# Which steps keep their G in PSUM: one fixed set against a set by the kind of half round

## The chip, the cores and the metric

The kernel runs on one core of a Trainium2 chip. The metric is the device time of one execution in microseconds; the time before is the median of three runs. The rows below come from one further execution, taken by the hardware profiler.

## What is computed

Agent attention followed by a feed-forward layer, all in float32. With `scale = 1/sqrt(128)` and B = 2, N = 12480 rows, C = 128, 49 agents, 2048 hidden units:

```python
def sm(a, b):
    s = scale * (a @ b.transpose(0, 2, 1))
    s = s - s.max(-1, keepdims=True)
    e = np.exp(s)
    return e / (e.sum(-1, keepdims=True) + 1e-09)
agent_v = sm(agents, k) @ v
x = (sm(q, agents) @ agent_v).reshape(B * N, C)
h = x @ w_in
g = np.where(h > 0.0, h, np.exp(np.minimum(h, 0.0)) - 1.0)
out = g @ w_out
```

## The kernel before

**Stages.** A prologue of some 57 us computes k's scores, the maximum, the exponentials and `agent_v` of the first batch and converts the weights. Then comes the main loop, which is the rest. It runs over S = 416 steps. A round is 960 rows of q (26 rounds, 13 in each batch); it has two half rounds of 480 rows, and a half round has NP = 8 steps, one for each 256 of the 2048 hidden units. So there are 52 half rounds, counted here from 0.

**One step s.** `p1` (L400) makes H for this step on TensorE, six matmuls of 480 columns into a tile `h` of two PSUM banks. `elu` (L411) computes `e = exp(h - 1)` on ScalarE (L414) and G = max(min(e, 1), h) on VectorE (L416). `split` (L419), called for the step before, splits G into two float32r parts for the product with `w_out`: `hi` on ScalarE (L202) and `lo = G - hi` (L207). `p2` (L432) is issued four steps later (LAG = 4), twelve matmuls that add into the two output banks; its last four pairs read `lo`.

**Kept steps.** If `is_kept(s)`, G is written back over H in the PSUM tile, and `lo` is one VectorE operation of 960 columns; the PSUM tile is then in use until that operation has ended. GpSimd reads only SBUF here, so in the other steps G goes to an SBUF tile `g` (three of them), the PSUM tile is free once VectorE has written G, and `lo` is two GpSimd operations of 480 columns. Before, steps 1, 3 and 6 of every half round are kept.

**PSUM tiles.** Two of the eight banks take the output, and six are three tiles of two banks that `slot` (L140) hands out. Everything else that needs PSUM in the main loop takes one of the same three.

**What else stands in a half round.** The next rounds' attention is spread over the steps by `plan` and `at` (L655, L474). A *visit* computes two pieces (scores of q, scores of k, or products with v) in one tile, which ScalarE and VectorE then read. Visits stand at step 1 (early) or at step 3 (late, EDGE = 3). Late ones are in half rounds 0, 1, 3, 5, ... 19, then 21, 25, 29, ... 45; early ones in 2, 4, ... 16. The transposes of the softmax of q (`q_ring`, L353) take a tile at step 6 of the even half rounds 2 to 48 (in half round 1 at step 4), which ScalarE (L346) and VectorE (`px`, L207) read. In half rounds without a late visit `p1` of step 5 is issued ahead, at step 4. The maximum over k takes a tile at step 5 of half round 8 and one at step 0 of half round 9. In half rounds 9 to 17 and 19, the maximum is subtracted (`e_sub`, L211, VectorE) or exponentials are taken for the second batch.

**Order.** Every engine runs its instructions in the order in which the loop at L724 issues them: in step s first `p1(s)`, then `p2(s - 4)`, `elu(s)`, `split(s - 1)`, and last the visit or the transposes of this step. The output is moved to HBM by SP's queue, which also loads the inputs.

Of the kernel before, what the change touches and what calls it, by code (L numbers as in the profile page):

```python
# [24 lines left out]
def tile_agent_attention_moe(  # L25
# [25 lines left out]
    LEAD = 6  # L51
    NP = NM // 2
    EDGE = (NP - 1 + LAG) % NP
    KEPT = (1, 3, 6)
    scale = 1.0 / float(C) ** 0.5

    const = ctx.enter_context(tc.tile_pool(name="const", bufs=1))
# [337 lines left out]
        return x // 2, x % 2, c  # L395

    def is_kept(s):
        return s % NP in KEPT

    def p1(s):  # L400
        j, half, c = at_step(s)
# [9 lines left out]
    def elu(s):  # L411

        h, e = h_t.pop(s), x_p.tile([128, 2, T], F32, tag="e", name="e")
        nc.scalar.activation(out=e, in_=h, func=ACTF.Exp, bias=-1.0, scale=1.0)  # L414
        g = h if is_kept(s) else g_p.tile([128, 2, T], F32, tag="g", name="g", bufs=3)
        nc.vector.scalar_tensor_tensor(out=g, in0=e, scalar=1.0, in1=h, op0=ALU.min, op1=ALU.max)  # L416
        g_t[s] = g

    def split(s):  # L419
        if not 0 <= s < S:  # L420
            return
        g = g_t.pop(s)
        hi_t[s] = hi = g_p.tile([128, 2, T], F32R, tag="hi", name="hi", bufs=5)
        lo_t[s] = lo = g_p.tile([128, 2, T], F32R, tag="lo", name="lo", bufs=4)
        cast_hi(nc.scalar, hi, g)
        if is_kept(s):
            rest(nc.vector, lo, g, hi)
        else:
            for i in range(2):
                rest(nc.gpsimd, lo[:, i, :], g[:, i, :], hi[:, i, :])  # L430
# [46 lines left out]
    with tc.manual_schedule():  # L477
# [153 lines left out]
        visits = {}  # L631
# [153 lines left out]
```

## Time and profile before

| | us |
|---|---|
| median of three runs (966.14 to 968.47) | 968.03 |
| the profiled execution | 964.99 |
| its span, first to last instruction | 963.2 |
| TensorE matmuls busy | 939.2 (98%) |
| ScalarE busy | 852.1 (88%) |
| VectorE busy | 786.7 (82%) |
| GpSimd busy | 726.5 (75%) |

Busy shares are means over the whole span, prologue included. The page's granted TensorE clock is 9 (90% or more) in each of its 40 slices. The matmuls of a step come in pairs that start together; the next pair starts 0.22 us later though each matmul is shown with 0.38. In the rows, PE is TensorE's matmuls, PEld its weight loads, DVE VectorE, ACT ScalarE, POOL GpSimd.

### The profile page before, as it was taken

How to read it: one execution, taken by the hardware profiler on the slowest of the kernel's cores; microseconds unless marked ns; L12 is line 12 of the kernel's file. 1: busy time of each engine (PE TensorE's matmuls, PEld its weight loads, DVE VectorE, ACT ScalarE, POOL GpSimd, SP SyncE). 2: the span in 40 equal slices, each digit the busy share in tenths (PEclk: the TensorE clock that was granted, in tenths of full speed). 3: DMA queues.
4: the chain of work that ended last, by engine and by line, in shares of the span. 5: the costliest groups of instructions: out<-in, count | busy, mean ns of one | idle time of the engine just before them, and what ended most of it. 6: DMA issues, size and time to landing. Idle time of an engine off the chain costs nothing.

```text
span 963.2 us, 26620 instructions
## 1 busy us (share of the span) xinstructions
PE 939.2 (98%) x11102; PEld 815.0 (85%) x11102; DVE 786.7 (82%) x897; ACT 852.1 (88%) x1020; POOL 726.5 (75%) x623
## 2 busy tenths in 40 slices
PE   7889999999999999999999999999999999999998
PEld 5778888888888888888888889888989888888886
DVE  7858788788888888888788888888888887888885
ACT  4649989988889889988999998999999999989996
POOL 3336777767877877877887887887878878878886
PEclk9989999999999999999999999999999999999999
DMA  9941222224232211012002101101020020001000
GB/s 347 400 145 55 103 95 78 69 74 121 67 92 82 68 33 59 27 38 73 28 21 69 38 27 53 38 28 63 28 78 28 22 68 31 31 15 38 27 22 21
DMA packets 26195, 67.48 MB, mean 70 GB/s; under 512 B 3239, under 2 KB 15171, under 8 KB 26075
## 3 DMA queue, kind: packets, MB, share of 16 engines
q1 hardware_dynamic: 26075, 65.79, 20.5%
q8 instruction: 87, 1.43, 0.6%
q14 instruction: 33, 0.27, 0.1%
HBM read 43.11 MB, written 12.78 MB: 58 GB/s over the span
## 4 chain that ended last, share of the span: by engine, by line
PE 68%; DVE 5%; ACT 2%; issue 2%; POOL 0%; DVEq 0%; ACTq 0%; POOLq 0%
PE o L444 43%; PE h L408 23%; ACT e L414 2%; PE h L222 1%; DVE g L416 1%; DVE lo L207 1%; DVE h L416 1%; DVE qe L307 1%; DVE mx L299 1%; PE h L332 0%; PE h L294 0%; ACT hi L202 0%; ACT oa L459 0%; DVE ob L456 0%; POOL ob L460 0%
## 5 line engine op out<-in xcount | busy, mean ns | idle before, releaser
L207 POOL TENSOR_TENSOR lo<-g,hi 128x480 fp32r<-128x480 f32 x520 | 627.1, 1238 | 137.7 <-PE h L408 68.5
L414 ACT ACTIVATE e<-h 128x960 f32<-128x960 f32 x416 | 406.1, 976 | 55.5 <-PE h L408 36.8
L416 DVE SCALAR_TENSOR_TENSOR g<-e,h 128x960 f32<-128x960 f32 x260 | 299.1, 1151 | 96.2 <-ACT e L414 94.4
L408 PE MATMUL h<-py,ahi 50*128 50x480 f32 x832 | 261.3, 394 | 5.1 <-DVE qe L307 3.2
L202 ACT ACTIVATE hi<-g 128x960 fp32r<-128x960 f32 x260 | 261.5, 1006 | 1.3 <-DVE g L416 1.3
L408 PE MATMUL h<-px,ahi 50*128 50x480 f32 x832 | 261.6, 394 | 0.9 <-DVE lo L207 0.5
L444 PE MATMUL o<-lo,w_hi 64*128 64x480 f32 x1664 | 255.1, 379 | 0.4 <-POOL lo L207 0.4
L444 PE MATMUL o<-hi,w_lo 64*128 64x480 f32 x1664 | 253.0, 377 | 1.3 <-ACT hi L202 1.3
L444 PE MATMUL o<-hi,w_hi 64*128 64x480 f32 x1664 | 254.3, 378 | 0.0
L416 DVE SCALAR_TENSOR_TENSOR h<-e,h 128x960 f32<-128x960 f32 x156 | 180.8, 1159 | 35.4 <-ACT e L414 31.3
L444 PEld LDWEIGHTS o<-lo,w_hi 64*128 64x128 f32 x1664 | 163.9, 184 | 20.4 <-POOL lo L207 1.2
L444 PEld LDWEIGHTS o<-hi,w_lo 64*128 64x128 f32 x1664 | 164.3, 185 | 19.8 <-ACT hi L202 1.4
L207 DVE TENSOR_TENSOR lo<-h,hi 128x960 fp32r<-128x960 f32 x156 | 179.4, 1150 | 0.0
L444 PEld LDWEIGHTS o<-hi,w_hi 64*128 64x128 f32 x1664 | 164.1, 184 | 17.4
L408 PEld LDWEIGHTS h<-py,ahi 50*128 50x128 f32 x832 | 145.1, 186 | 26.0 <-PE o L444 6.2
L408 PEld LDWEIGHTS h<-px,ahi 50*128 50x128 f32 x832 | 145.2, 186 | 16.7 <-DVE g L416 5.4
L408 PE MATMUL h<-py,alo 49*128 49x480 f32 x416 | 156.9, 377 | 0.0
L408 PE MATMUL h<-px,alo 49*128 49x480 f32 x416 | 156.9, 377 | 0.0
L202 ACT ACTIVATE hi<-h 128x960 fp32r<-128x960 f32 x156 | 151.6, 971 | 0.0
L460 POOL TENSOR_TENSOR ob<-ob,oa 128x480 f32<-128x480 f32 x51 | 63.4, 1243 | 58.6 <-ACT oa L459 38.8
L408 PEld LDWEIGHTS h<-px,alo 49*128 49x128 f32 x416 | 78.1, 188 | 4.9 <-DVE alo L278 0.2
L408 PEld LDWEIGHTS h<-py,alo 49*128 49x128 f32 x416 | 78.2, 188 | 4.7
(98 smaller groups left out, 523.0 us busy)
## 6 DMA issues: line engine op xcount, KB each, us to landing
k<-in_kT_dram SPq DMA_DIRECT2D x26, 480.0 KB
q<-in_qT_dram SPq DMA_DIRECT2D x26, 480.0 KB
out_dram<-ob SPq DMA_DIRECT2D x51, 240.0 KB
v<-in_vx_dram SPq DMA_DIRECT2D x13, 516.0 KB
v<-in_vx_dram SPq DMA_DIRECT2D x13, 483.8 KB
py<-px SPq DMA_DIRECT2D x52, 93.8 KB
py<-px SPq DMA_DIRECT2D x52, 91.9 KB
raw<-in_w_in_dram SPq DMA_DIRECT2D x4, 512.0 KB
```

What stands on the lines that cost most here:

```text
L202: nc.scalar.activation(out=out, in_=x, func=ACTF.Copy)
L207: eng.tensor_tensor(out=out, in0=x, in1=hi.bitcast(F32), op=ALU.subtract)
L222: nc.tensor.matmul(out=ps[u:u + 64], lhsT=e[:, j * NA:j * NA + 64], rhs=v_t[b, r][:, j, :], start=(r == rs[0] and j < 2), stop=(r == rs[-1 ...
L299: nc.vector.tensor_reduce(out=mx, in_=v, axis=AX.X, op=ALU.max)
L307: nc.vector.tensor_tensor(out=e, in0=v, in1=q_st[j]["mx"].unsqueeze(2).to_broadcast([TQ, R, NA]), op=ALU.subtract)
L408: nc.tensor.matmul(out=h[:, u, 0:T], lhsT=a[x, :], rhs=p[u ^ half][x, :], start=i == 0, stop=i == 2)
L414: nc.scalar.activation(out=e, in_=h, func=ACTF.Exp, bias=-1.0, scale=1.0)
L416: nc.vector.scalar_tensor_tensor(out=g, in0=e, scalar=1.0, in1=h, op0=ALU.min, op1=ALU.max)
L444: nc.tensor.matmul(out=o_t[u][:, 0:T], lhsT=w[x], rhs=v[x, :], start=first and i == 0, stop=last and i == len(jobs) - 1)
L460: nc.gpsimd.tensor_tensor(out=ob, in0=ob, in1=oa, op=ALU.add)
```

## The change

The fixed set of kept steps becomes a table by the kind of half round, and `is_kept` looks up the kind: "late" if a visit stands at step 3, else "early" if one stands at step 1, else "turn" in even half rounds (those with transposes and no visit), else none. `visits` is filled before the loop runs. In late half rounds steps 1 and 6 are kept, step 3 no longer; in early and turn half rounds 1, 3 and 7; in the others 1, 3 and 6 as before.

```diff
-    KEPT = (1, 3, 6)
+    KEPT = {"late": (1, 6), "early": (1, 3, 7), "turn": (1, 3, 7), None: (1, 3, 6)}
@@
     def is_kept(s):
-        return s % NP in KEPT
+        first = s - s % NP
+        steps = visits.values()
+        if first + EDGE in steps:
+            kind = "late"
+        elif first + 1 in steps:
+            kind = "early"
+        else:
+            kind = "turn" if first // NP % 2 == 0 else None
+        return s - first in KEPT[kind]
```

## Rows read from the trace of the kernel before

**Rows 1.** The page: busy us, share of the span, instructions, of each engine

```profile
PE 939.2 (98%) x11102; PEld 815.0 (85%) x11102; DVE 786.7 (82%) x897; ACT 852.1 (88%) x1020; POOL 726.5 (75%) x623
```

**Rows 2.** The page: the chain that ended last, shares by engine

```profile
PE 68%; DVE 5%; ACT 2%; issue 2%; POOL 0%; DVEq 0%; ACTq 0%; POOLq 0%
```

**Rows 3.** Half rounds 27, 24, 25: stretch, length, busy us (instructions) by engine

```profile
541.76:557.72 15.96, 15.96 (x146) 13.57 (x146) 13.39 (x14) 15.29 (x19) 12.49 (x11) 1.00 0.12 40
...
491.37:507.51 16.14, 16.14 (x155) 13.59 (x152) 13.43 (x13) 15.66 (x20) 14.72 (x14) 1.00 0.04 16
507.51:525.61 18.10, 17.71 (x274) 15.69 (x274) 15.43 (x18) 16.03 (x20) 13.14 (x12) 1.00 0.29 92
```

**Rows 4.** Half round 25, two q: start, us, engine, operation [idle before, releaser]

```profile
511.48 0.37 PE L408 MATMUL h<-py,ahi 50*128 50x480 f32 x1
...
513.44 0.37 PE L408 MATMUL h<-py,ahi 50*128 50x480 f32 x1
...
516.21 1.15 DVE L416 SCALAR_TENSOR_TENSOR h<-e,h 128x960 f32<-128x960 f32 x1
...
517.02 0.48 PE L408 MATMUL h<-py,ahi 50*128 50x480 f32 x1
...
517.61 2.38 POOL L207 TENSOR_TENSOR lo<-g,hi 128x480 fp32r<-128x480 f32 x2
...
518.92 0.96 ACT L202 ACTIVATE hi<-h 128x960 fp32r<-128x960 f32 x1
...
518.94 0.56 DVE L307 TENSOR_TENSOR qe<-h,mx 124x392 f32<-124x392 f32 x1
...
519.65 0.45 PE L408 MATMUL h<-py,ahi 50*128 50x480 f32 x1 [0.39 <-DVE qe L307]
...
522.67 4.79 POOL L207 TENSOR_TENSOR lo<-g,hi 128x480 fp32r<-128x480 f32 x4 [2.68 <-ACT hi L202]
```

**Rows 5.** What `p1` (L408) waited for, loads and matmuls: us, times

```profile
  DVE px L207: 4.7, 21
...
  DVE qe L307: 3.2, 8
```

**Rows 6.** Half round 1: `p1` of steps 4 and 5

```profile
87.38 0.48 PE L408 MATMUL h<-py,ahi 50*128 50x480 f32 x1
...
90.81 0.48 PE L408 MATMUL h<-py,ahi 50*128 50x480 f32 x1 [0.53 <-DVE g L416]
```

**Rows 7.** The page's costliest groups: count, busy us, mean ns, idle before

```profile
L207 POOL TENSOR_TENSOR lo<-g,hi 128x480 fp32r<-128x480 f32 x520 | 627.1, 1238 | 137.7 <-PE h L408 68.5
...
L408 PE MATMUL h<-py,ahi 50*128 50x480 f32 x832 | 261.3, 394 | 5.1 <-DVE qe L307 3.2
...
L207 DVE TENSOR_TENSOR lo<-h,hi 128x960 fp32r<-128x960 f32 x156 | 179.4, 1150 | 0.0
```

**Rows 8.** Half round 3, q and k: `p1` of steps 4 and 5

```profile
124.67 0.48 PE L408 MATMUL h<-py,ahi 50*128 50x480 f32 x1
...
127.14 0.46 PE L408 MATMUL h<-py,ahi 50*128 50x480 f32 x1 [0.22 <-DVE m_all L171]
```

**Rows 9.** `lo` of steps 4, 5 in half round 24; matmuls reading step 6's

```profile
504.57 4.79 POOL L207 TENSOR_TENSOR lo<-g,hi 128x480 fp32r<-128x480 f32 x4 [0.74 <-POOL lo L207]
...
513.00 0.60 PE L444 MATMUL o<-lo,w_hi 64*128 64x480 f32 x4
```

**Rows 10.** Half round 9: G of step 0, and `p1` of step 1

```profile
226.81 1.14 DVE L416 SCALAR_TENSOR_TENSOR g<-e,h 128x960 f32<-128x960 f32 x1
...
226.94 0.48 PE L408 MATMUL h<-py,ahi 50*128 50x480 f32 x1
```

**Rows 11.** Half round 11: subtractions (L211), and GpSimd's `lo` beside the second

```profile
269.66 0.56 DVE L211 TENSOR_TENSOR s_all<-s_all,mb 120x392 f32<-120x392 f32 x1
...
276.60 1.02 DVE L211 TENSOR_TENSOR s_all<-s_all,mb 120x392 f32<-120x392 f32 x1
...
275.97 5.54 POOL L207 TENSOR_TENSOR lo<-g,hi 128x480 fp32r<-128x480 f32 x4 [2.30 <-ACT hi L202]
```

## The prediction

> **What bounds the kernel now.** I read the page's busy shares first, then the chain that ended last, then the busy time of single half rounds, then the order of time inside a few of them. TensorE is busy 98% of the span [rows 1] and the chain runs through its matmuls [rows 2]. So a microsecond in which TensorE stands still after the prologue is a microsecond of the span, and other engines count only where they make it stand. A half round (8 steps) with nothing in it takes 15.96 us [rows 3]. A plain step is 1.96 us, from one `p1` to the next at 511.48 and 513.44 [rows 4], and 8 of those are 15.7: such a half round has almost nothing to win. One with transposes takes 16.14 and TensorE is busy in all of it. One with a late visit of two q parts takes 18.10, and there TensorE is busy for 17.71, so 0.4 us idle [rows 3].
>
> The idle time has a name. After the late visit at step 3 comes `p1` of step 4 at 517.02, then `p1` of step 5 only at 519.65. That is 2.63 us where 1.96 is plain, and it waits for `qe` (L307), the last reader of the visit's PSUM tile, 518.94 + 0.56 [rows 4]. The three PSUM tiles are handed out by who is released first in program order. With step 3 kept, its tile is released only by its `lo` on VectorE in step 4, so the earliest released tile for step 5 is the visit's own, and its four VectorE operations come behind step 3's `g`. The trace fits that order elsewhere too: the `p1` behind the transposes waits for `px` (L207), their tile's last reader, 21 times [rows 5], and in half round 1, where the transposes come at step 4, step 5 waits for step 4's `g` [rows 6].
>
> **What the change moves.** Of 52 half rounds, 18 have a late visit, 8 an early visit, 17 are "turn", 9 are the rest. The kept steps go from 156 to 18 x 2 + 34 x 3 = 138. Eighteen `lo` leave VectorE (18 x 1.150 = 20.7 us) and come to GpSimd as 36 operations of 1.238 us (44.6 us) [rows 7]. In 25 even half rounds the third kept step moves from 6 to 7, with no change in counts. No DMA is added or moved on SP's queue.
>
> **Late visit without step 3.** I walked the hand-out of tiles through one such half round. The visit still takes step 2's tile, step 4 still takes step 1's (released by step 1's `lo`), but step 5 now takes step 3's, which step 3's `g` releases: 516.21 + 1.15 = 517.36 [rows 4], 1.6 us before it is wanted. The visit's tile goes to step 6, wanted at about 521 and free at 519.50. So the wait goes wholly. The price of one: 2.63 - 1.96 = 0.67, less about 0.1 by which the first matmul after a visit is longer anyway (0.48 at 517.02, 0.37 at 511.48 [rows 4]); I take 0.6. The trace has this wait for `qe` 8 times [rows 5]: 8 x 0.6 = 4.8 us. With q and k the same step waits for the k reduction: 127.14 - 124.67 = 2.47, so 0.51 - 0.1, about 0.45 [rows 8], in half rounds 0, 3, 5 and 7: 1.8 us. In half round 1 the step from 87.38 to 90.81 is 3.43 [rows 6]; less 1.96, 0.1 and 0.2 for the transposes (16.14 - 15.96 [rows 3]), some 1.1 remains, and by the new order both the transposes and step 5 get tiles that are free in time: 1.0 us. The five other late half rounds (11, 13, 15, 17, 19) show no such wait and give nothing. Sum: 4.8 + 1.8 + 1.0 = 7.6 us. The low bound is TensorE's own idle before these: 3.2 for the eight `qe` [rows 5], 0.53 in half round 1 [rows 6], 0.22 for each q and k [rows 8], some 4.6 us.
>
> What hides the added GpSimd work: step 2's `lo` ends at 517.61 + 2.38 = 519.99, step 3's `hi` at 518.92 + 0.96 = 519.88, and GpSimd then stands idle 2.68 us until step 4's `hi` [rows 4]. The new pair, 2.4 us, fits that hole. If it did not, step 4's and 5's `lo` would be late by what sticks out, and `p2` four steps later would wait. In the whole half round GpSimd would be busy 13.14 + 2.4 = 15.5 of about 17.5 us [rows 3].
>
> **Transposes or early visit, step 7 for 6.** Behind the transposes, step 0 of the next half round now takes step 6's tile (released by its `g`, before the transposes' readers), so the wait for `px` goes: 4.7 us of weight loads in 21 places [rows 5]. The loads run ahead of their matmuls, and of those the costliest group of this line shows only 5.1 us idle in all, 3.2 of it `qe` [rows 7]. So the gain lies between 0 and 4.7; I take 1.0, near the low end. GpSimd now has steps 4, 5, 6 in a row: steps 4 and 5 end at 504.57 + 4.79 = 509.36, step 6 would end at 511.8, and the matmuls that read it start at 513.00 [rows 9]: 1.2 us of slack, no stall. VectorE does step 7's `lo` in step 0 instead of step 6's in step 7. It stands behind step 0's `g` there, so `g` of step 1 moves by some 0.3 us, which nobody on TensorE waits for.
>
> One place loses. In half round 9 the second small matmul of the k maximum takes a tile in step 0. It now takes the transposes' tile, and `p1` of step 1 gets step 0's own, so it waits for step 0's `g`. That starts at 226.81 today and could start some 0.25 earlier (its `e` is done by then), ending near 227.65, while `p1` starts at 226.94 [rows 10]: +0.7 us, once.
>
> **Contention.** In the half rounds that subtract the maximum (`s_all`, L211, both inputs in SBUF) one such operation took 0.56 us at 269.66 and another 1.02 at 276.60, in the middle of four `lo` on GpSimd that took 5.54 us [rows 11] where four take 4.79 elsewhere [rows 9]. So they collide, by 0.75 us on GpSimd and 0.46 on VectorE in such a half round, whereas the `lo` of a kept G keeps a mean of 1.15 us and GpSimd's 1.24 [rows 7]. In five late half rounds the added GpSimd pair lies next to those subtractions. TensorE waits for no `lo` there today, so I take 0, and keep half of the 0.75 in each, 5 x 0.4 = 2 us, for the range.
>
> The Trainium skill (SBUF — State Buffer, Who interferes with whom) has the rule: a VectorE instruction with two SBUF inputs and a GpSimd instruction that reads SBUF exclude each other for the whole instruction, while one with at most one SBUF input doesn't contend. By it, moving a `lo` from VectorE, where G came from PSUM, to GpSimd speaks against the change: free work becomes work that can be blocked. The rows agree on both halves of the rule. By it the sum would lose up to the 2 us kept above.
>
> **Sum.** 7.6 + 1.0 - 0.7 = 7.9 us. Against the profiled execution: span 963.2, so 955.3, and its time 964.99 gives 957.1. The median of the runs shown is 968.03, 3.0 above the profiled execution, so I set the sum against the median: 960.1, rounded to 960.
>
> **Rivals.**
> (1) *The stall comes back later in the half round.* After the visit ScalarE has `e`, `hi` and the exponentials of q back to back; were step 5's `e` late, step 6 or 7 would inherit part of the wait. For: ScalarE is busy 16.03 of 18.10 there [rows 3]. Against: the tiles that steps 6 and 7 take are released over 1.5 us before. Half of the 7.6 stays: 964.
> (2) *The change doesn't do what it says:* the tiles are handed out otherwise than I read, so step 5 still gets the visit's. Then 7.6 falls away and the rest nearly cancels: 968. Against: three different waits in the trace fit my reading [rows 4 to 6].
> (3) *GpSimd becomes the bound:* slower. A late half round with an even one after it (18.10 + 16.14 = 34.2 us) holds 13.14 + 14.72 = 27.9 us of GpSimd today, with 2.4 more 30.3 [rows 3], in 22 `lo` operations and others. It decides where one operation takes (34.2 - 30.3) / 22 = 0.18 us above its 1.2. Beside L211 four of them took 5.54, so 1.385 each [rows 11], just there. If the moved `lo` of step 7 collided as L211 does, with 1.45 each (0.25 x 22 = 5.5), the pair would take 35.8, 1.6 more than today, in some 15 pairs: about 992. Against: kept and unkept `lo` run side by side today at their usual times.
>
> **How the numbers follow.** Forecast 960: 0.70, within 956.5 to 963 by the bounds above (4.6 instead of 7.6, 0 to 4.7 for `px`, 2 us of contention). Rival 1, 964: 0.11. Rival 2, 968: 0.11. Rival 3, 992: 0.08. A range from 956.5 to 966 holds the forecast and rival 1, 0.8. A measurement of this kernel tells some 0.3% (2.9 us) from no change. Faster by more: the forecast and nearly all of rival 1, 0.80; within: rival 2 and a little of rival 1, 0.12; slower: 0.08.
>
> **What would show it.** Right: in a late half round with two q parts the step from `p1` 4 to `p1` 5 falls from 2.63 to about 2.07 and the half round from 18.1 to about 17.5; TensorE's wait for `qe` is gone; after transposes the wait for `px` is gone; GpSimd has no hole of 2.7 us after a late visit; `p2` never waits for `lo`. In half round 9 a new wait of some 0.7 us on `g`. Wrong: late half rounds still at 18 us, or `p1`, `p2` waits on GpSimd's `lo`, or GpSimd operations over 1.3 us on the mean.

## The result and the profile after

The changed kernel takes 958.08 us, the median of six runs (956.81 to 961.22), where the kernel before took 967.44 in its six (966.1 to 969.24). The ratio is 0.9908, with a 95% interval of 0.9886 to 0.9930: 8.9 us faster, between 6.8 and 11.0.

The profiled execution of the changed kernel took 960.39 us, its span is 958.6, so the span is only 4.6 us shorter than that of the kernel before (963.2). Where the rest is, the first start of `p1` tells, which ends the prologue. These are the rows for one group of `p1`'s matmuls, before and after (count, ns least/median/most, first and last start in us; line 416 after is line 408 before):

```profile
L408 PE MATMUL h<-px,ahi x832: 372/380/598, 57.3 to 951.8; 50*128 50x480 f32 x84, 49*128 49x480 f32 x83
```

```profile
L416 PE MATMUL h<-px,ahi x832: 372/380/766, 60.6 to 947.2; 50*128 50x480 f32 x84, 49*128 49x480 f32 x83
```

The main loop, from there to the end of the span, took 963.2 - 57.3 = 905.9 us before and 958.6 - 60.6 = 898.0 after: 7.9 us less. The prologue, which the change doesn't touch, was 3.3 us longer in this execution. The last section shows that it varies from execution to execution, and main loops are compared below by this difference.

Half round 0 opens the main loop, and its length varies too, by over 1 us with the same work, as the experiment on the even half rounds shows. These are the stretches behind it, before and after (length, then busy us and instructions of PE, PEld, DVE, ACT, POOL, then clock, DMA share, GB/s):

```profile
77.40:963.20 885.80, 875.73 (x10129) 762.52 (x10125) 732.39 (x788) 810.91 (x951) 701.76 (x591) 1.00 0.17 51
```

```profile
80.83:958.60 877.77, 871.72 (x10129) 768.84 (x10125) 715.08 (x771) 807.68 (x951) 742.66 (x625) 1.00 0.17 52
```

That is 8.0 us less behind half round 0.

On the page after (busy us and share of the span by engine; then the chain that ended last), GpSimd has gained 43 us and VectorE lost 18 against [rows 1], near the 44.6 and 20.7 that were forecast for 36 operations more and 18 fewer:

```profile
PE 939.0 (98%) x11102; PEld 825.1 (86%) x11102; DVE 769.1 (80%) x879; ACT 848.8 (89%) x1020; POOL 769.4 (80%) x659
...
PE 93%; DVE 2%; ACT 2%; POOL 1%; DMA 1%; issue 0%; SPq 0%; DVEq 0%; ACTq 0%; POOLq 0%
```

Over the whole span the busy time of TensorE is the same to 0.2 us, but only because the longer prologue makes up for the rest: behind half round 0 it fell from 875.7 to 871.7 us, and the idle time from 10.1 to 6.1. So half of the 8.0 us was standing still by the profile, and half was shown as busy time. The two shares of matmuls in the chain, 68% [rows 2] and 93%, can't be set side by side: before, the chain could be followed back only to 211.9 us, and its shares add up to 77%. From some 260 us on, where both chains are known, matmuls are about 90% of the one before and all of the one after.

The stretches after, half rounds 25, 24, 27, 9 and 11, in the same columns:

```profile
507.71:525.22 17.51, 17.51 (x275) 16.25 (x273) 14.35 (x17) 15.88 (x20) 15.28 (x14) 1.00 0.29 95
491.62:507.71 16.09, 16.09 (x154) 15.22 (x152) 13.40 (x13) 15.63 (x19) 14.69 (x14) 1.00 0.04 16
541.36:557.24 15.88, 15.88 (x147) 13.97 (x145) 13.40 (x14) 15.24 (x19) 12.54 (x11) 1.00 0.12 40
225.81:243.92 18.11, 17.18 (x212) 14.97 (x210) 14.75 (x19) 15.81 (x20) 13.67 (x12) 1.00 0.45 118
...
262.38:280.23 17.85, 17.85 (x226) 15.11 (x224) 14.95 (x18) 16.23 (x22) 15.55 (x13) 1.00 0.32 92
```

Against [rows 3], the half round with a late visit of two q parts falls from 18.10 to 17.51 and TensorE is busy in all of it; the turn half round and the plain one hardly move (0.05 and 0.08). Inside half round 25 (start, us, engine, operation, idle before):

```profile
516.42 1.15 DVE L424 SCALAR_TENSOR_TENSOR g<-e,h 128x960 f32<-128x960 f32 x1
...
517.26 0.48 PE L416 MATMUL h<-py,ahi 50*128 50x480 f32 x1
...
517.82 9.59 POOL L207 TENSOR_TENSOR lo<-g,hi 128x480 fp32r<-128x480 f32 x8
...
519.14 0.57 DVE L307 TENSOR_TENSOR qe<-h,mx 124x392 f32<-124x392 f32 x1
...
519.33 0.38 PE L416 MATMUL h<-px,ahi 50*128 50x480 f32 x1
...
521.30 0.37 PE L416 MATMUL h<-px,ahi 50*128 50x480 f32 x1
```

Step 5's `p1` now starts at 519.33, 2.07 us after step 4's, while the visit's last reader (`qe`) runs until 519.71: it no longer waits for it. Step 6's, which by the walk has the visit's tile, comes at 521.30, 1.6 us after that. GpSimd has no hole: eight `lo` operations stand in one row where 2.68 us were idle [rows 4], at the same 1.2 us each.

Everything that `p1` waits for after, loads and matmuls together (us, times), in place of [rows 5]:

```profile
its engine sat idle before it (us, times) until:
  DVE g L424: 10.6, 39
  issue: 3.2, 13
  ACT e L422: 1.6, 4
  DVE lo L207: 1.2, 2
  ACT ahi L270: 0.9, 2
  DMA py<-px: 0.5, 1
  DVE alo L278: 0.2, 1
```

The two waits that carried the sum, `qe` (3.2 us, 8 times) and `px` (4.7 us, 21 times), have no row any more. A new one, for a DMA (a copy by the DMA engines), has.

### The profile page after: what moved, and what is told of

It is laid out like the page before. It is cut to its first block, busy times and chain, and to the rows that moved or that the text cites. A ratio compares the mean times of both kernels' runs of the same rounds, so it can differ in the third digit from the quotient of the medians.

```text
span 958.6 us, 26706 instructions
## 1 busy us (share of the span) xinstructions
PE 939.0 (98%) x11102; PEld 825.1 (86%) x11102; DVE 769.1 (80%) x879; ACT 848.8 (89%) x1020; POOL 769.4 (80%) x659
## 3 DMA queue, kind: packets, MB, share of 16 engines
q1 hardware_dynamic: 26075, 65.79, 20.7%
## 4 chain that ended last, share of the span: by engine, by line
PE 93%; DVE 2%; ACT 2%; POOL 1%; DMA 1%; issue 0%; SPq 0%; DVEq 0%; ACTq 0%; POOLq 0%
PE o L452 55%; PE h L416 29%; PE h L222 3%; PE h L294 2%; PE h L163 1%; POOL lo L207 1%; DMA k<-in_kT_dram 1%; PE h L332 1%; DVE g L424 0%; DVE m_all L171 0%; DVE ex L110 0%; PE h L478 0%; ACT ex L106 0%; DMA py<-px 0%; DVE fr L112 0%
## 5 line engine op out<-in xcount | busy, mean ns | idle before, releaser
L207 POOL TENSOR_TENSOR lo<-g,hi 128x480 fp32r<-128x480 f32 x556 | 669.9, 1239 | 82.2 <-ACT hi L202 36.2
L424 DVE SCALAR_TENSOR_TENSOR g<-e,h 128x960 f32<-128x960 f32 x278 | 320.1, 1152 | 122.5 <-ACT e L422 93.7
L202 ACT ACTIVATE hi<-g 128x960 fp32r<-128x960 f32 x278 | 279.6, 1006 | 1.3 <-DVE g L424 1.3
L424 DVE SCALAR_TENSOR_TENSOR h<-e,h 128x960 f32<-128x960 f32 x138 | 159.8, 1158 | 19.0 <-ACT e L422 16.9
L416 PEld LDWEIGHTS h<-px,ahi 50*128 50x128 f32 x832 | 147.5, 186 | 16.1 <-DVE g L424 5.4
L416 PEld LDWEIGHTS h<-py,ahi 50*128 50x128 f32 x832 | 147.5, 186 | 15.5 <-DVE g L424 4.1
L207 DVE TENSOR_TENSOR lo<-h,hi 128x960 fp32r<-128x960 f32 x138 | 158.8, 1151 | 0.0
L202 ACT ACTIVATE hi<-h 128x960 fp32r<-128x960 f32 x138 | 134.0, 971 | 0.2 <-DVE h L424 0.2
```

What stands on the lines that cost most here:

```text
L202: nc.scalar.activation(out=out, in_=x, func=ACTF.Copy)
L207: eng.tensor_tensor(out=out, in0=x, in1=hi.bitcast(F32), op=ALU.subtract)
L416: nc.tensor.matmul(out=h[:, u, 0:T], lhsT=a[x, :], rhs=p[u ^ half][x, :], start=i == 0, stop=i == 2)
```

## The experiments

The ratios below are to the kernel before, timed beside each kernel, and main loops are span less first `p1`. Edits are shown against the changed kernel. The main loop is the sharper measure: it was 898.0 and 898.2 us for the changed kernel in two executions, while single times of one kernel spread over 3 to 7 us. It still holds half round 0, so "behind half round 0" gives it without that one: 885.8 us before, 877.8 and 877.9 for the changed kernel in its two executions.

**Late half rounds alone.**

```diff
-    KEPT = {"late": (1, 6), "early": (1, 3, 7), "turn": (1, 3, 7), None: (1, 3, 6)}
+    KEPT = {"late": (1, 6), "early": (1, 3, 6), "turn": (1, 3, 6), None: (1, 3, 6)}
```

> Only the late half rounds change (steps 1 and 6 kept); the even ones keep 1, 3, 6 as before. Theory (the wait for the visit's PSUM tile at step 5 is what the change removes): nearly all of the gain, 7.4 us, so a ratio near 0.992; the step from p1 4 to p1 5 in a late half round with two q is 2.07 us instead of 2.63; half round 9 loses nothing, since step 7 of half round 8 isn't kept. Rival (the even half rounds bring the gain by lifting the wait for px): under 2 us, ratio above 0.998.

Measured: ratio 0.9934 (0.9916 to 0.9952). Main loop 954.6 - 56.1 = 898.5 us, 7.4 less than before; behind half round 0 878.6, 7.2 less. Of its waits of `p1` (us, times) this one is left of the two:

```profile
  DVE px L207: 4.8, 21
```

and this is half round 9, in the columns of the stretches above:

```profile
221.17:238.36 17.19, 17.17 (x212) 14.65 (x210) 14.72 (x19) 15.82 (x20) 13.73 (x12) 1.00 0.46 125
```

So the wait for `px` is still there in full, that for `qe` has gone, and nearly the whole gain is there. Half round 9 takes 17.19, not 18.11.

**Even half rounds alone.**

```diff
-    KEPT = {"late": (1, 6), "early": (1, 3, 7), "turn": (1, 3, 7), None: (1, 3, 6)}
+    KEPT = {"late": (1, 3, 6), "early": (1, 3, 7), "turn": (1, 3, 7), None: (1, 3, 6)}
```

> Only the even half rounds change (1, 3, 7 kept); the late ones keep 1, 3, 6. Theory: some 20 waits for px give 0.05 to 0.1 us each and two after the second batch's weights 0.3 each, 2 us in all, and half round 9 loses 0.9: a net gain near 1 us, ratio 0.998 to 1.000. Rival (VectorE's lo in step 0 delays the next half round): no gain or a loss, ratio above 1.000, with waits on g at step 1 or 2 of odd half rounds.

Measured: ratio 0.9992 (0.9978 to 1.0005), no change that the times can tell. Main loop 963.3 - 59.3 = 904.0 us, 1.9 less, but 1.2 of it is half round 0, in which this kernel issues the same work: 18.87 us instead of 20.11, at a granted clock of 0.91 instead of 0.83. These rows are half round 0 before:

```profile
57.29:77.40 20.11, 18.27 (x240) 14.54 (x242) 14.53 (x20) 13.24 (x16) 6.42 (x6) 0.83 0.26 85
```

and half rounds 0 and 9 of this kernel:

```profile
59.31:78.18 18.87, 16.90 (x241) 13.08 (x243) 14.53 (x20) 13.12 (x16) 6.43 (x6) 0.91 0.16 54
...
225.27:244.12 18.85, 17.42 (x213) 14.89 (x211) 16.05 (x20) 16.12 (x20) 12.57 (x11) 1.00 0.42 114
```

Of the two waits of `p1` it is now the other that is left:

```profile
  DVE qe L307: 3.5, 8
```

So the even half rounds are worth 0.7 us net (885.1 behind half round 0): the wait for `px` has gone, that for `qe` stays, and half round 9 has grown from 17.94 us to 18.85. Behind half round 0 the two parts add up, 7.2 + 0.7 = 7.9, to what the change gives together, 8.0.

**Step 4 kept instead of step 3 in late half rounds.** This leaves VectorE as many `lo` as before the change, but frees step 3's tile early.

```diff
-    KEPT = {"late": (1, 6), "early": (1, 3, 7), "turn": (1, 3, 7), None: (1, 3, 6)}
+    KEPT = {"late": (1, 4, 6), "early": (1, 3, 7), "turn": (1, 3, 7), None: (1, 3, 6)}
```

> As the change, but in late half rounds step 4 is kept in place of step 3 (1, 4, 6), so VectorE does as many lo there as before the change. Theory (whose PSUM tile is free for step 5): step 3's tile is still released by its g, so the step from p1 4 to p1 5 stays at 2.07 and the ratio is 0.991, as of the change. Rival (what helps is 20.7 us of lo taken off VectorE behind the visit): the late half rounds keep some 18.1 us and the ratio is 0.999 or above. GpSimd has 36 operations fewer than in the change.

Measured: ratio 0.9927 (0.9912 to 0.9942), main loop 960.5 - 60.5 = 900.0 us. `p1` of steps 4 and 5 of half round 25:

```profile
519.36 0.48 PE L416 MATMUL h<-py,ahi 50*128 50x480 f32 x1
...
521.42 0.38 PE L416 MATMUL h<-py,ahi 50*128 50x480 f32 x1
```

and the half round's stretch:

```profile
507.64:525.08 17.44, 17.44 (x280) 15.97 (x278) 14.76 (x17) 15.93 (x20) 14.88 (x13) 1.00 0.29 94
```

The step is 2.06 us and the half round 17.44, as in the change or a little better, with the VectorE work of the kernel before. So it is the tile and not VectorE's load that counted. The time as a whole is 2.0 us longer in the main loop than the change's, which was not expected: step 4's tile is now the late one. 0.8 us of it stand in half round 19, where the second batch's sum takes a tile at step 5 and the next `p1` waits 0.83 us for `g`. Another 0.8 stand in half round 0, where `p1` of step 7 now waits for `g` too and comes 1.46 us after step 6's, which takes 0.66 in the nine other profiles:

```profile
79.51 0.48 PE L416 MATMUL h<-px,ahi 50*128 50x480 f32 x1 [0.63 <-DVE g L424]
```

The early half rounds 10 to 16 lose 1.1 together, with new waits of weight loads for `g` at their start, and half round 1 gains 0.5.

**Steps 1 and 6 kept everywhere**, which does without the kinds.

```diff
-    KEPT = {"late": (1, 6), "early": (1, 3, 7), "turn": (1, 3, 7), None: (1, 3, 6)}
+    KEPT = {"late": (1, 6), "early": (1, 6), "turn": (1, 6), None: (1, 6)}
```

> Steps 1 and 6 kept in all half rounds: step 3's lo on GpSimd everywhere. Theory: the late half rounds gain as in the change, 7.4 us, and the others have nothing to win from it, while GpSimd there gets steps 2 to 5 in a row behind q_mul and ob: matmuls wait for lo in the turn half rounds (busy 14.7 + 2.4 = 17.1 of 16.1 us), some 0.3 to 1 us each in 34 half rounds, 10 to 30 us lost, so slower than the change, ratio 1.00 to 1.02. Rival (GpSimd has room everywhere and the kinds aren't needed): ratio 0.990 to 0.993.

Measured: ratio 0.9949 (0.9932 to 0.9966), main loop 958.9 - 57.0 = 901.9 us, 3.9 more than the change: between the two theories, and the loss much smaller than I expected. Late half rounds do as well as in the change (17.58 for number 25). The loss is where the half rounds are short, and in the last one. GpSimd and the weight loads around the start of turn half round 24, and the matmuls at the end of the kernel, in order of time:

```profile
481.57 10.73 POOL L207 TENSOR_TENSOR lo<-g,hi 128x480 fp32r<-128x480 f32 x9
...
491.17 0.19 PEld L452 LDWEIGHTS o<-lo,w_hi 64*128 64x128 f32 x2 [0.45 <-POOL lo L207]
...
949.18 0.49 PE L452 MATMUL o<-lo,w_hi 64*128 64x480 f32 x2 [0.27 <-POOL lo L207]
...
951.52 0.49 PE L452 MATMUL o<-lo,w_hi 64*128 64x480 f32 x2 [0.67 <-POOL lo L207]
```

Half round 24's stretch:

```profile
487.25:503.67 16.42, 16.38 (x155) 13.53 (x152) 12.48 (x12) 15.67 (x20) 16.42 (x15) 1.00 0.04 16
```

In the plain half round before (15.9 us) GpSimd has steps 2 to 5 in a row from 481.57, and step 5's `lo` comes 0.45 us too late for its weight load; GpSimd is busy in all of the 16.42 us of half round 24 (the change has 14.69 of 16.09). The turn half rounds with such a wait lose 0.2 to 0.3 us each, 2.3 together, and the last half round 1.8. The other differences about cancel: the wait for `px` is back (7.2 us in 23 weight loads and matmuls), and half round 9 is short again. A late half round is 1.6 us longer than a plain one, and in number 25 the same row of work fits. The kind of the half round does matter, for GpSimd's sake.

**Half round 8 with 1, 3, 6.**

```diff
+        if first == 8 * NP:
+            kind = None
         return s - first in KEPT[kind]
```

> The change, but half round 8, the only one whose next half round takes a PSUM tile for the k maximum at step 0, keeps 1, 3, 6. Theory (step 7 kept there makes p1 of step 1 in half round 9 wait for step 0's g): half round 9 falls from 18.11 to about 17.2 us and nothing else moves, 0.9 us in all, ratio near 0.990. Rival (half round 9 is long for the added lo on GpSimd beside the subtractions): it stays at 18.1.

Measured: ratio 0.9906 (0.9886 to 0.9926); main loop 959.1 - 62.0 = 897.1 us, 0.9 less than the change (876.8 behind half round 0, 1.0 less). Half round 9 is short again:

```profile
227.41:244.62 17.21, 17.19 (x213) 14.73 (x210) 14.76 (x19) 15.84 (x20) 13.69 (x12) 1.00 0.46 124
```

It is the best version by its main loop; by its times it can't be told from the change.

**A longer visit, in the kernel before and in the changed one.** The maximum of a q part is taken twice, into the same place, one VectorE operation more for each of 25 parts. The new function `q_again`, left out here, repeats the reduction of `q_max` into the same `mx`.

```diff
@@
                 if kind == "q":
                     q_max(n)
+                    q_again(n)
                     q_sub(n)
```

In the kernel before:

> The kernel before with the maximum of each q part of a visit taken twice (one more VectorE operation of 0.56 us, 25 in all). Theory (step 5's tile is the visit's, so each VectorE operation on the visit is on TensorE's path): the step from p1 4 to p1 5 grows by 1.1 us with two q (7 half rounds) and by 0.56 with one and k, and by somewhat less with e: 7.8 + 3.4 + 2 = 13 us, ratio about 1.013. Rival (the wait hangs on VectorE's total work, 14 us more of 787): under 3 us, ratio below 1.004.

Measured: ratio 1.0149 (1.0126 to 1.0171), main loop 982.9 - 60.8 = 922.1 us, 16.2 more than before (15.5 behind half round 0), where 13 were expected. `p1` of steps 4 and 5 in half round 25:

```profile
529.51 0.48 PE L412 MATMUL h<-py,ahi 50*128 50x480 f32 x1
...
533.34 0.45 PE L412 MATMUL h<-py,ahi 50*128 50x480 f32 x1 [1.60 <-DVE qe L311]
```

The wait in all (us, times) was 3.2 in [rows 5] and is now:

```profile
  DVE qe L311: 12.3, 8
```

In the changed kernel:

> The changed kernel with the same extra operation. Theory (the visit's tile goes to step 6, 1.5 us after it is free): the extra 0.56 or 1.1 us stays within that slack, the step from p1 4 to p1 5 stays at 2.07 and the time is that of the change within 2 us, ratio 0.990 to 0.993. Rival (the wait has only moved): it grows as in the kernel before, by some 10 us, ratio about 1.00.

Measured: ratio 0.9943 (0.9924 to 0.9962), main loop 955.5 - 57.0 = 898.5 us, 0.5 more than the change; behind half round 0 878.7, 0.9 more. `p1` of steps 4 and 5:

```profile
513.95 0.48 PE L420 MATMUL h<-py,ahi 50*128 50x480 f32 x1
...
516.02 0.38 PE L420 MATMUL h<-px,ahi 50*128 50x480 f32 x1
```

The same 1.1 us of VectorE work on the visit's tile lengthens the step from 2.63 to 3.83 us in the one kernel and leaves it at 2.07 in the other. This is the plainest of the experiments on the cause. The time of the changed kernel with it missed my bound: its ratio lies above 0.993, though its main loop in the profile is only 0.5 to 0.9 us longer. What the timed runs have there and the profiled one lacks stays open.

**The change once more,** beside these three:

> The changed kernel once more, beside the others on the same chip: ratio 0.989 to 0.993; the main loop again 893.8 us in the profile, and the prologue between 56 and 61 us, as it was in the kernels run so far whatever they changed.

Measured: ratio 0.9909 (0.9890 to 0.9928); 959.6 - 61.4 = 898.2 us of main loop, 0.2 more than in the first execution. The 893.8 of the expectation is no main loop in this measure, and no profile of the changed kernel gives it. The prologue was 0.4 us longer than the longest expected.

## Why the prediction was right

The forecast was 960 us, 7.9 less than the median then known; measured were 958.08, a ratio that stands for 8.9 us less, and 7.9 us less in the main loops of the two profiles. The mechanism was right; that the sum agrees to the tenth is luck, since terms that were too small and losses that were not foreseen cancel.

*The wait after the late visit* was the term that mattered, 7.6 us. The kernel with the late half rounds alone gives 7.4, or 7.2 behind half round 0. By the lengths of its half rounds the eight waits for `qe` gave 5.3 us where 4.8 were put, half round 1 gave 1.0 as put, and half rounds 3, 5 and 7 gave 1.3, about the 0.45 each that was put. The 0.45 of half round 0 can't be seen: its step from `p1` 4 to `p1` 5 took 2.46 us before, 2.33 with the late half rounds alone and 2.67 in the change. The low bound of 4.6 counted idle time alone. Half of what the change gained had been shown as busy time, so the price by the length of the steps was the right one. The step I read out of [rows 4] fell from 2.63 to 2.07 us, which is the 2.07 named beforehand. Where the tiles go was the mechanism; the longer visit and the kept step 4 show it from two sides. That five late half rounds had nothing to win was right: with the late half rounds alone, half round 11 takes 17.95 us. Before it took 17.94:

```profile
260.86:278.80 17.94, 17.94 (x226) 15.50 (x226) 15.95 (x20) 16.27 (x22) 13.33 (x12) 1.00 0.32 92
```

*The wait for `px`* was put at 1.0 us between 0 and 4.7. Alone, with the loss in half round 9, the even half rounds gave 0.7; with that loss of 0.9 added back the gain there is 1.6. So the term was 0.6 too small. 0.6 of the 1.6 came from the turn half rounds 20 and 22 (0.3 each), in which the second batch's weights take a tile at step 7; half rounds 21 and 23 behind them gave 0.2 each back in the change, a place that the walk left out.

*The loss in half round 9* was put at 0.7 and was 0.9: 18.11 with step 7 of half round 8 kept, 17.21 without. The rows show the wait that was named, step 0's `g` and then step 1's `p1`, in place of [rows 10]:

```profile
227.81 1.16 DVE L424 SCALAR_TENSOR_TENSOR g<-e,h 128x960 f32<-128x960 f32 x1 [0.89 <-ACT e L422]
...
229.02 0.48 PE L416 MATMUL h<-py,ahi 50*128 50x480 f32 x1 [0.93 <-DVE g L424]
```

The half round begins at 225.81 here and at 224.64 before. Taken back by these 1.17 us, `g` starts at 226.64 and `p1` at 227.85; I had `g` end near 227.65 and `p1` start there, 0.2 too early.

*What I had not seen* is half round 2. Half round 1 became 1.0 us shorter, as forecast, but its transposes stand at step 4 and `p1` of half round 2 reads their copies, which DMAs move between partitions. Issuing them took 3.1 us before and after, but the first is issued 5.1 us before half round 2 begins, where it was 5.9. So a weight load now waits for them:

```profile
99.92 0.18 PEld L416 LDWEIGHTS h<-py,ahi 49*128 49x128 f32 x1 [0.49 <-DMA py<-px]
```

Some 0.4 us are lost there (18.67 us where 18.24 stood before). The step that failed is the walk through half round 1: it followed the tiles up to the moment the transposes were early and didn't ask who needs their result and by what way it comes. Together with the 0.2 in half round 9 this takes back what `px` gave more. A second loss that I had not seen is half round 10, in the next paragraph.

*GpSimd* did what [rows 4] and [rows 9] let expect: one operation takes 1.239 us on the mean (1.238 before [rows 7]), it is busy 15.28 of 17.51 us in half round 25 (15.5 of 17.5 forecast). Beside the subtractions little was lost. Half round 11, where [rows 11] come from, is no longer than before. But half round 9 now starts nine `lo` in a row, and they took 11.46 us where nine at the mean take 11.15; a subtraction in their midst took 0.85 where one took 0.56 [rows 11]. A weight load in half round 10 then waits for the `lo` of half round 9's step 5:

```profile
237.43 11.46 POOL L207 TENSOR_TENSOR lo<-g,hi 128x480 fp32r<-128x480 f32 x9
...
241.78 0.85 DVE L211 TENSOR_TENSOR s_all<-s_all,mb 120x392 f32<-120x392 f32 x1
...
247.76 0.19 PEld L452 LDWEIGHTS o<-lo,w_hi 64*128 64x128 f32 x2 [0.37 <-POOL lo L207]
```

Half round 10 takes 18.46 us where it took 18.28, 18.49 with the late half rounds alone and 18.27 with the even ones alone. So `p2` does wait for `lo` once because of the change, and for the contention, which was put at 0 with 2 us as its bound, the longer row with the collision in it cost some 0.2 us. No run separates the collision from the row. The Trainium skill (SBUF — State Buffer, Who interferes with whom) has a VectorE instruction with two SBUF inputs contend with a GpSimd instruction that reads SBUF. These rows agree.

*The rivals.* The stall did not come back: `p1` of steps 5 and 6 follows at 2.07 and 1.97 us. The change does what it says. GpSimd did not become the bound, but the kernel with 1 and 6 everywhere shows how near it is: there a plain half round's `lo` came 0.45 us late. That kernel's main loop is 3.9 us longer than the change's, and its half rounds with late `lo` account for it. The price of 992 us that I gave this rival rested on operations of 1.45 us, and their mean was 1.239; the wait comes where four steps in a row meet a short half round.

## What to carry to other kernels

Where few buffers are handed out by who is released first, ask for each stalled allocation which buffer it got and why the others were not free; keeping one tile a step less can free TensorE even where the work moves to a slower engine. Walk the new hand-out through every special place, and follow each producer that becomes earlier to its reader. Whether the slower engine can carry the work is decided stretch by stretch: the same row of work fitted a half round of 17.5 us and not one of 15.9.

## What the runs showed of the hardware

The prologue of this kernel was 56.1 to 62.0 us long in ten profiles, whatever had been changed in the main loop. In general it is the longer, the lower the mean clock that TensorE was granted in it, though at a mean of 0.94 it was anything from 57.0 to 59.3. The stretch from the start to the first `p1`, in the kernel with late half rounds alone and in the one with half round 8 changed (the value after the five busy times is the mean granted clock, as a share of 2.4 GHz):

```profile
0.00:56.10 56.10, 43.89 (x735) 36.63 (x735) 40.16 (x90) 27.98 (x55) 18.23 (x27) 0.97 0.95 361
```

```profile
0.00:62.00 62.00, 51.61 (x735) 44.55 (x735) 39.56 (x90) 28.08 (x55) 17.86 (x27) 0.81 0.88 338
```

The same 735 matmuls keep TensorE busy for 43.89 us at a mean of 0.97 and for 51.61 at 0.81; part of the stretch ran at the lower level of 1.2 GHz. Half round 0 shows the same with the same work: 18.87 us at 0.91 and 20.11 at 0.83, in the rows of the experiment on the even half rounds. The page of the kernel before has it as an 8 in the third of its 40 slices; only the other 39 are 9, where the text ahead gives 9 for all. In the prologue of the kernel before, TensorE was busy for 7.69 of the 10 us from 20 to 30 at a clock of 1.00; from 30 to 40 the mean was 0.83, and from 40 to 50, busy for 9.79, it was 1.00 again. That the clock is the cause and not a companion wasn't tested. For a change of 8 us this is no small thing: these ten executions, which share the prologue's code, differ by up to 5.9 us before the changed part begins.
